# First layer's spatial products in other banks, newest norm first, last token tiles one by one

## The chip, the cores and the metric

The kernel runs on one core of one Trainium2 chip. The metric is the device time of one execution in microseconds (us). A core has five engines with instruction streams of their own: TensorE (PE, with its weight loads PEld), VectorE (DVE), ScalarE (ACT), GpSimd (POOL) and SyncE (SP), which here issues nearly all DMAs. Matmuls write to PSUM, which is dealt out in banks of 128 x 512 float32. VectorE and ScalarE read results from there ("evict" them) and so free the bank for a later matmul.

## The reference, cut to what matters

Sigmoid attention over 4 batches, 12 heads, 448 tokens and head size 64, then two gated layers with a spatial product (d_model 768, two halves of 512 features).

```python
scores = scale * np.matmul(q, k.transpose(0, 1, 3, 2)) - np.log(S)
x = np.matmul(1.0 / (1.0 + np.exp(-scores)), v)      # then heads side by side: (4, 448, 768)

# a gated layer; the first has relu and no g, the second gelu, g and "+ x" around the result
h = act(x @ w_in)                                    # (4, 448, 1024)
u, v = h[..., :512], h[..., 512:]
v_n = (v - mean(v)) / np.sqrt(var(v) + 1e-06) * g    # over the 512 features of a token
v_s = np.einsum('ts,bsd->btd', w_spatial, v_n) + b_spatial[None, :, None]
out = (u * v_s) @ w_out                              # (4, 448, 768)
```

## The kernel before, in words

Float32 products are made of three products of rounded parts: each operand is a high part (written by ScalarE's copy) and a low part (VectorE subtracts the high part from the value), and high x high, high x low, low x high are added up in one PSUM bank.

The work on TensorE has these stages, in the order of the program: attention; the first layer, batch by batch; a product of the first layer's `w_out` and the second layer's `w_in` ("merge", in place of two products later); the second layer, batch by batch. In a layer a batch b goes through

- `hv(b, j)` for 4 token tiles (3 in odd batches; the rests of 64 tokens of two batches share one tile): the v half of h, for 128 tokens and 512 features. 18 matmuls of 512 columns in the first layer, 12 in the second. ScalarE evicts the bank with the activation (L594), VectorE takes mean and variance (L597, L598), GpSimd makes 1/sqrt (L599, L602). The rest, `norm`, is put on a list of jobs, `chain`.
- `norm` (a generator): at its second tick VectorE applies mean and factor (L608) and ScalarE copies the high part (L616, or L622 for the tile of rests); at its third tick VectorE makes the low part (L618, L625).
- `hu(b, i)` for 4 blocks of 128 features: the u half, turned, 12 matmuls of 448 columns in the second layer and 18 in the first; ScalarE evicts (L639).
- `sp(b, i)` for the same 4 blocks: 11 matmuls of the spatial product (L654). In the first layer VectorE adds the bias (L658) and multiplies with u (L660); in the second it does so at L664 and L668, then ScalarE copies the high part (L672) and VectorE makes the low one (L682).
- in the second layer `out(b, i, False)` and `out(b, i, True)`: what x and what block i of the gated product give to the turned output, over six banks (`out_banks`: two pairs "sc" and two banks "av"). In the last batch `out_last` makes the output in token rows instead: three token tiles k = 1, 2, 3, each in a bank of 512 and one of 256 columns, and `rests_first`/`rests_last` make the tile of rests of two batches in the banks "t". `leave` copies a finished token tile out of PSUM and writes it with a DMA.

Banks: `bank()` deals from a pool "t" of two, `av_bank()` from a pool "av" of two, `two_banks()` from a pool "sc" of two pairs. A matmul into a bank waits until the last result there is evicted.

Order: all engines' instructions stand in the order in which this program issues them. After each product a step is made (`fill` in the first layer, `step` in the second). It ticks three belts of jobs: `chain` (the norms and low parts), `spatial` (loads of spatial weights) and `belt` (loads of other weights). `Belt.tick` goes through its running jobs in the order in which they were added, so the oldest norm comes first. In the second layer a step first calls `store`: VectorE transposes one of the six banks of the batch before (L797) and SP writes it out; a batch has six, one per step from its first.

Of the kernel before, what the change touches and what calls it, by code (L numbers as in the profile page):

```python
# [26 lines left out]
def tile_sigmoid_attention_two_gated_mlps(  # L27
# [36 lines left out]
    P = 128  # L64
# [5 lines left out]
    KF = FF // P  # L70
# [22 lines left out]
    def bank():  # L93
        return later["ps_t"].tile([P, 512], F32, tag="t", name="t")

    def two_banks():
        return later["ps_sc"].tile([P, 2, 512], F32, tag="sc", name="sc")

    def av_bank():
        return ps_av.tile([P, 512], F32, tag="av", name="av")  # L100
# [162 lines left out]
    class Belt:  # L263


        def __init__(self):
            self.waiting, self.running = [], []

        def add(self, job):
            self.running.append(job)  # L270

        def tick(self, new=0):
            for job in list(self.running):
                if next(job, self) is self:
                    self.running.remove(job)
            while new and self.waiting:
                job = self.waiting.pop(0)
                next(job)
                self.running.append(job)
                new -= 1  # L280
# [30 lines left out]

    first = pieces_in(l1)
    out1 = pieces_kept(w_out1, 0, rows_of(flat))
    belt, chain, spatial = Belt(), Belt(), Belt()
    spatial.waiting = [load_w_sp(l1, j) for j in range(4)]


# [241 lines left out]
    class Mlp:  # L559
# [82 lines left out]
        def sp(self, b, i):  # L642
            L = self.L
            cols = slice(REST, SPAN) if b % 2 == 0 else slice(0, S)
            fs = slice(i * P, (i + 1) * P)
            ps = av_bank() if L.n == 1 and i % 2 else bank()
            todo = []
            for j in range(3):
                (vh, vl), wh, wl = self.v[j], L.sh[:, j, cols], L.sl[:, j, cols]
                todo += [(vh[:, fs], wh), (vh[:, fs], wl), (vl[:, fs], wh)]  # L650
            vr = self.v[3][b % 2]
            todo += [(vr[:, fs], w[:, 3, cols]) for w in (L.sh, L.sl)]
            for n, (a, w) in enumerate(todo):
                nc.tensor.matmul(ps[:, :S], a, w, start=(n == 0), stop=(n == len(todo) - 1))  # L654
            u = self.u[i]
            t = self.pool.tile([P, S + 16], F32, tag="gt", name="gt", bufs=1)[:, :S]
            if L.n == 1:
                nc.vector.tensor_tensor(out=t, in0=ps[:, :S], in1=L.bb[:, cols], op=ALU.add)  # L658
                o = (b % 2) * S
                nc.vector.tensor_tensor(  # L660
                    out=xs[b // 2][:, i, o:o + S], in0=t, in1=u, op=ALU.mult
                )
                return
            nc.vector.scalar_tensor_tensor(  # L664
                out=t, in0=ps[:, :S], scalar=L.gc[:, i:i + 1], in1=L.bb[:, cols],
                op0=ALU.mult, op1=ALU.add,
            )
            nc.vector.tensor_tensor(out=u, in0=t, in1=u, op=ALU.mult)  # L668
            whole, rest = self.parts(b)
            gh = self.pool.tile([P, S], F32R, tag="gh", name="gh", bufs=2)  # L670
            gl = self.pool.tile([P, S], F32R, tag="gl", name="gl", bufs=2)
            nc.scalar.copy(out=gh[:, whole], in_=u[:, whole])  # L672
            self.g[i] = gh, gl
            if rest:
                if b % 2 == 0:
                    self.rests[i] = stg.tile([P, 2, P], F32R, tag="f", name="gr", bufs=4)
                at = REST * (b % 2)
                rh, rl = [self.rests[i][:, x, at:at + REST] for x in range(2)]
                nc.scalar.copy(out=rh, in_=u[:, rest])

            def low():
                nc.vector.tensor_tensor(  # L682
                    out=gl[:, whole], in0=u[:, whole], in1=raw(gh[:, whole]), op=ALU.subtract
                )
                if rest:
                    nc.vector.tensor_tensor(out=rl, in0=u[:, rest], in1=raw(rh), op=ALU.subtract)
                yield

            chain.add(low())
# [44 lines left out]

        ends = slice(0, 512), slice(512, DM)

        def out_last(self, b, i, second):


            if not second and i == 0:  # L740
                self.out_banks()
            pair = self.g.pop(i) if second else self.x[b][i]
            done = second and i == KF - 1
            for k in range(1, 4):
                at = REST + (k - 1) * P
                bs = self.o[2 * (k - 1):2 * k]
                for ps, cols in zip(bs, self.ends):
                    self.rows(ps, [x[:, at:at + P] for x in pair], i, second, cols)
                    if done and k == 3:
                        self.leave(k, [(ps, cols)], ((out[b, (k - 1) * P:k * P], slice(0, P)),))  # L750
                if done and k < 3:
                    row = out[b, (k - 1) * P:k * P]
                    self.leave(k, zip(bs, self.ends), ((row, slice(0, P)),), both=k)

        def rests_first(self, b):

# [80 lines left out]
    with tc.manual_schedule():  # L837
# [23 lines left out]
        with tc.tile_pool(name="fpool", bufs=1) as fpool:  # L861
# [106 lines left out]
            for b in range(B):  # L968
                last = b == B - 1
                stores = list(range(KD)) if b else []  # L970

                def step(new=0, waits=False):
                    if stores:
                        m2.store(b - 1, stores.pop(0))
                    fill(0 if b else new, waits)

                def split_next(c):
                    if not last:
                        m2.split_x(b + 1, c, c + 1)

                out_part = m2.out_last if last else m2.out
                for j in range(4 - b % 2):
                    m2.hv(b, j)
                    step(1)
                for i in range(KF):
                    m2.hu(b, i)
                    step(2)
                m2.sp(b, 0)
                step(1, True)
                m2.sp(b, 1)  # L990
                step(1, True)
                out_part(b, 0, False)
                split_next(0)
                step(1)
                out_part(b, 0, True)
                split_next(1)
                step(1)
                m2.sp(b, 2)
                step(0, True)
                out_part(b, 1, False)  # L1000
                split_next(2)
                step(1)
                out_part(b, 1, True)
                split_next(3)
                step()
                m2.sp(b, 3)
                step(0, True)
                out_part(b, 2, False)
                step()
                out_part(b, 2, True)  # L1010
                out_part(b, 3, False)
                if last:
                    m2.rests_first(b)
                    m2.rests_last(b)
                out_part(b, 3, True)


# [33 lines left out]
```

## Time and profile before

| | |
|---|---|
| Median of 3 runs | 563.37 us (563.28 to 563.59) |
| The profiled execution | 563.3 us |
| Its span, first to last instruction | 561.5 us |
| TensorE busy | 552.6 us, 98% of the span |
| VectorE busy | 367.7 us, 65% |
| ScalarE busy | 231.8 us, 41% |
| GpSimd busy | 30.3 us, 5% |
| Mean granted TensorE clock | 0.999 |

TensorE's row of busy time includes the drain of each matmul, which overlaps the next matmul, so its length says less than the distance between the starts of two matmuls. In a timeline the bracket behind a row is the idle time of its engine before it and what ended it. The chain of waits lists what the last instruction had to wait for, in order of time; "issue" pieces are left out below.

### The profile page before, as it was taken

How to read it: one execution, taken by the hardware profiler on the slowest of the kernel's cores; microseconds unless marked ns; L12 is line 12 of the kernel's file. 1: busy time of each engine (PE TensorE's matmuls, PEld its weight loads, DVE VectorE, ACT ScalarE, POOL GpSimd, SP SyncE). 2: the span in 40 equal slices, each digit the busy share in tenths (PEclk: the TensorE clock that was granted, in tenths of full speed). 3: DMA queues.
4: the chain of work that ended last, by engine and by line, in shares of the span. 5: the costliest groups of instructions: out<-in, count | busy, mean ns of one | idle time of the engine just before them, and what ended most of it. 6: DMA issues, size and time to landing. Idle time of an engine off the chain costs nothing.

```text
span 561.5 us, 9207 instructions
## 1 busy us (share of the span) xinstructions
PE 552.6 (98%) x3484; PEld 438.1 (78%) x3484; DVE 367.7 (65%) x835; ACT 231.8 (41%) x389; POOL 30.3 (5%) x62
## 2 busy tenths in 40 slices
PE   8999999999999999999999999999999999999996
PEld 6444444444799898897998888998999879989885
DVE  5999999875589799889774977942541264225211
ACT  6878878876342261351542245311320132112001
POOL 0000000000110200200100020001000110010000
PEclk9999999999999999999999999999999999999999
DMA  7868677533044265552545534101500140014003
GB/s 221 234 188 229 166 223 211 150 68 72 4 139 132 68 171 119 128 144 87 160 143 121 140 116 127 58 0 19 81 1 0 22 78 1 1 20 66 0 1 112
DMA packets 96893, 56.45 MB, mean 101 GB/s; under 512 B 67537, under 2 KB 84049, under 8 KB 96849
## 3 DMA queue, kind: packets, MB, share of 16 engines
q1 hardware_dynamic: 96704, 55.60, 37.9%
q8 instruction: 27, 0.44, 0.3%
q10 hardware_dynamic: 144, 0.26, 0.1%
q14 instruction: 18, 0.14, 0.1%
HBM read 44.83 MB, written 11.01 MB: 99 GB/s over the span
## 4 chain that ended last, share of the span: by engine, by line
PE 93%; DVE 2%; ACT 2%; DMA 1%; issue 0%; SPq 0%; DVEq 0%
PE t L634 16%; PE t L588 15%; PE av L457 13%; PE sc L720 10%; PE t L654 9%; PE sc L423 9%; PE av L720 5%; PE av L654 3%; PE sc L730 3%; PE t L814 3%; PE av L814 3%; PE sc L441 2%; PE t L730 1%; PE av L730 1%; DMA inq<-in_q_dram 1%; DVE st L597 1%
## 5 line engine op out<-in xcount | busy, mean ns | idle before, releaser
L408 ACT ACTIVATE a<-sc,small 128x896 f32<-128x896 f32 x72 | 68.6, 1007 | 20.5 <-PE sc L423 20.5
L597 DVE BATCH_NORM_STATS2 st<-vr 128x6 f32<-128x512 f32 x28 | 19.4, 694 | 67.4 <-ACT vr L594 67.4
L457 PE MATMUL av<-a,vt 128*64 128x448 f32 x288 | 63.2, 554 | 0.0
L423 PEld LDWEIGHTS sc<-opq,opk 32*128 32x128 f32 x864 | 40.2, 183 | 26.3 <-issue 8.5
L423 PE MATMUL sc<-opq,opk 32*128 32x448 f32 x864 | 55.4, 378 | 0.2 <-ACT opq L382 0.2
L594 ACT ACTIVATE vr<-t 128x512 f32<-128x512 f32 x28 | 16.7, 597 | 90.9 <-PE t L588 87.6
L654 PE MATMUL t<-sh,v 128*128 128x448 f32 x168 | 49.2, 362 | 0.0
L588 PE MATMUL t<-vh,xh 128*128 128x512 f32 x112 | 41.6, 391 | 0.7 <-ACT vr L594 0.7
L457 PEld LDWEIGHTS av<-a,vt 128*64 128x64 f32 x288 | 17.0, 136 | 31.9 <-issue 28.4
L664 DVE SCALAR_TENSOR_TENSOR gt<-t,bb 128x448 f32<-128x448 f32 x16 | 10.9, 682 | 46.1 <-PE t L654 46.1
L672 ACT CAST gh<-u 128x448 fp32r<-128x448 f32 (+1 forms) x16 | 8.6, 540 | 71.6 <-DVE u L668 71.6
L588 PE MATMUL t<-vh,xl 128*128 128x512 f32 x98 | 38.1, 389 | 0.0
L599 POOL TENSOR_SCALAR st<-st 128x1 f32<-128x1 f32 x28 | 10.7, 382 | 473.9 <-DVE st L598 473.9
L634 PE MATMUL t<-xh,uh 128*128 128x448 f32 x96 | 34.9, 363 | 0.0
L634 PE MATMUL t<-xh,ul 128*128 128x448 f32 x96 | 34.8, 362 | 0.0
L654 PE MATMUL t<-sl,v 128*128 128x448 f32 x96 | 34.7, 362 | 0.0
L634 PE MATMUL t<-xl,uh 128*128 128x448 f32 x96 | 34.6, 360 | 0.0
L654 PEld LDWEIGHTS t<-sh,v 128*128 128x128 f32 x168 | 31.5, 187 | 2.0
L616 ACT CAST v<-vr 128x512 fp32r<-128x512 f32 x24 | 14.9, 621 | 43.8 <-DVE vr L608 43.8
L588 PE MATMUL t<-vl,xh 128*128 128x512 f32 x84 | 32.7, 389 | 0.0
L182 DVE SCALAR_TENSOR_TENSOR f<-w,f 128x256 uint32<-128x256 uint32 x72 | 30.6, 425 | 2.5
L188 DVE SCALAR_TENSOR_TENSOR f<-w,f 128x256 int32<-128x256 int32 x72 | 30.6, 425 | 2.4
(196 smaller groups left out, 1253.8 us busy)
## 6 DMA issues: line engine op xcount, KB each, us to landing
w<-in_moe_w_in_dram SPq DMA_DIRECT2D x48, 256.0 KB, 3.5
w<-in_moe_w_out_dram SPq DMA_DIRECT2D x24, 256.0 KB, 3.1
ink<-in_k_dram SPq DMA_DIRECT2D x12, 448.0 KB, 5.9
inq<-in_q_dram SPq DMA_DIRECT2D x12, 448.0 KB, 7.4
vt<-in_v_dram SPq DMA_DIRECT2D x48, 96.0 KB, 6.6
out_dram<-y SPq DMA_DIRECT2D x48, 56.0 KB, 1.9
flat<-f SPq DMA_DIRECT2D x18, 128.0 KB, 1.7
w<-flat SPq DMA_DIRECT2D x12, 192.0 KB, 2.4
```

The lines of the kernel that those rows point to most:

```text
L182: nc.vector.scalar_tensor_tensor(out=f.bitcast(U32), in0=low.bitcast(U32), scalar=29, in1=f.bitcast(U32), op0=ALU.logical_shift_right, op1 ...
L188: nc.vector.scalar_tensor_tensor(out=f, in0=high, scalar=-0x40000000, in1=f, op0=ALU.bitwise_and, op1=ALU.bitwise_or)
L408: nc.scalar.activation(a[:, 2 * x:2 * x + 2], sc[x][:, :, :S], AF.Sigmoid, bias=bias_s, scale=scale)
L423: nc.tensor.matmul(sc[h // 2][:, h % 2, :S], opk[ps, x, o:o + P], opq[ps, y, S * j:S * (j + 1)], start=(t == 0), stop=(t == 5), tile_posit ...
L457: nc.tensor.matmul(avp[n, x][o * D:(o + 1) * D, :S], vt[:, h, r] if r < 3 else vr[ps, o], att[n, r][:, h] if r < 3 else att[n, r][ps, h], ...
L588: nc.tensor.matmul(ps[:, :FF], a, w, start=(c == 0 and n == 0), stop=(c == self.kc - 1 and n == 2),)
L597: nc.vector.bn_stats(out=st, in_=vr)
L634: nc.tensor.matmul(ps[:, :S], w, a, start=(c == 0 and n == 0), stop=(c == self.kc - 1 and n == 2),)
L654: nc.tensor.matmul(ps[:, :S], a, w, start=(n == 0), stop=(n == len(todo) - 1))
L720: nc.tensor.matmul(self.o[m][:, :n_cols], w, a, start=(not second and i == 0 and n == 0), stop=(second and i == KF - 1 and n == 2),)
L730: nc.tensor.matmul(ps[:, :cols.stop - cols.start], a, w, start=(not second and i == 0 and n == 0), stop=(second and i == KF - 1 and n == 2),)
L814: nc.tensor.matmul(ps[:, :FF], x, w[:, c], start=(c == 0 and n == 0), stop=(c == KD - 1 and n == 2),)
```

## The change

Four edits:

- `sp` in the first layer takes "sc" (the first bank of a pair) for blocks 0 and 2, where it took "t"; blocks 1 and 3 take "av" as before. The second layer's `sp` still takes "t".
- `chain` is a `Belt(-1)`: a tick goes through the running jobs from the newest to the oldest.
- `step` in the second layer calls `fill` first and `store` behind it. Two stores stand in the first step of a batch, none in the other steps of `hv`, one in each step of `hu`.
- In the last batch `out_last(b, 3, False)` and the rests come ahead of the last two blocks of the gated product, and these two are taken together, token tile by token tile: tile 1 is finished, then 2, then 3.

```diff
--- before.py
+++ after.py
@@ -263,14 +263,14 @@
     class Belt:
 
 
-        def __init__(self):
-            self.waiting, self.running = [], []
+        def __init__(self, order=1):
+            self.waiting, self.running, self.order = [], [], order
 
         def add(self, job):
             self.running.append(job)
 
         def tick(self, new=0):
-            for job in list(self.running):
+            for job in self.running[::self.order]:
                 if next(job, self) is self:
                     self.running.remove(job)
             while new and self.waiting:
@@ -311,7 +311,7 @@
 
     first = pieces_in(l1)
     out1 = pieces_kept(w_out1, 0, rows_of(flat))
-    belt, chain, spatial = Belt(), Belt(), Belt()
+    belt, chain, spatial = Belt(), Belt(-1), Belt()
     spatial.waiting = [load_w_sp(l1, j) for j in range(4)]
 
 
@@ -643,7 +643,7 @@
             L = self.L
             cols = slice(REST, SPAN) if b % 2 == 0 else slice(0, S)
             fs = slice(i * P, (i + 1) * P)
-            ps = av_bank() if L.n == 1 and i % 2 else bank()
+            ps = bank() if L.n == 2 else av_bank() if i % 2 else two_banks()[:, 0]
             todo = []
             for j in range(3):
                 (vh, vl), wh, wl = self.v[j], L.sh[:, j, cols], L.sl[:, j, cols]
@@ -734,23 +734,25 @@
 
         ends = slice(0, 512), slice(512, DM)
 
-        def out_last(self, b, i, second):
+        def out_last(self, b, i, second, more=()):
 
 
             if not second and i == 0:
                 self.out_banks()
-            pair = self.g.pop(i) if second else self.x[b][i]
-            done = second and i == KF - 1
+            steps = ((i, second), *more)
+            done = steps[-1] == (KF - 1, True)
+            pairs = [self.g[i] if second else self.x[b][i] for i, second in steps]
             for k in range(1, 4):
                 at = REST + (k - 1) * P
+                row = ((out[b, (k - 1) * P:k * P], slice(0, P)),)
                 bs = self.o[2 * (k - 1):2 * k]
                 for ps, cols in zip(bs, self.ends):
-                    self.rows(ps, [x[:, at:at + P] for x in pair], i, second, cols)
+                    for pair, s in zip(pairs, steps):
+                        self.rows(ps, [x[:, at:at + P] for x in pair], *s, cols)
                     if done and k == 3:
-                        self.leave(k, [(ps, cols)], ((out[b, (k - 1) * P:k * P], slice(0, P)),))
+                        self.leave(k, [(ps, cols)], row)
                 if done and k < 3:
-                    row = out[b, (k - 1) * P:k * P]
-                    self.leave(k, zip(bs, self.ends), ((row, slice(0, P)),), both=k)
+                    self.leave(k, zip(bs, self.ends), row, both=k)
 
         def rests_first(self, b):
 
@@ -969,10 +971,11 @@
                 last = b == B - 1
                 stores = list(range(KD)) if b else []
 
-                def step(new=0, waits=False):
-                    if stores:
-                        m2.store(b - 1, stores.pop(0))
+                def step(new=0, waits=False, n=0):
                     fill(0 if b else new, waits)
+                    for c in stores[:n]:
+                        m2.store(b - 1, c)
+                    del stores[:n]
 
                 def split_next(c):
                     if not last:
@@ -981,10 +984,10 @@
                 out_part = m2.out_last if last else m2.out
                 for j in range(4 - b % 2):
                     m2.hv(b, j)
-                    step(1)
+                    step(1, n=0 if j else 2)
                 for i in range(KF):
                     m2.hu(b, i)
-                    step(2)
+                    step(2, n=1)
                 m2.sp(b, 0)
                 step(1, True)
                 m2.sp(b, 1)
@@ -1007,11 +1010,14 @@
                 step(0, True)
                 out_part(b, 2, False)
                 step()
+                if last:
+                    out_part(b, 3, False)
+                    m2.rests_first(b)
+                    m2.rests_last(b)
+                    out_part(b, 2, True, ((3, True),))
+                    continue
                 out_part(b, 2, True)
                 out_part(b, 3, False)
-                if last:
-                    m2.rests_first(b)
-                    m2.rests_last(b)
                 out_part(b, 3, True)
 
 
```

First TensorE, in the first layer around the end of batch 2: the first matmuls of the spatial products of blocks 0 and 2, and of the first three v-products of batch 3, with what they wait for. Before:

```order
L654 MATMUL t_3353<-sh1_1956,v0_3066 128x448 [waits Activation_49]
...
L654 MATMUL t_3394<-sh1_1956,v0_3066 128x448 [waits Activation_49]
...
L588 MATMUL t_3429<-vh1_79,xh_3246 128x512 [waits DVE_49]
...
L588 MATMUL t_3471<-vh1_79,xh_3246 128x512 [waits Activation_49]
...
L588 MATMUL t_3512<-vh1_79,xh_3246 128x512 [waits DVE_49]
```

and in the changed kernel:

```order
L654 MATMUL sc_3353<-sh1_1956,v0_3066 128x448
...
L654 MATMUL sc_3394<-sh1_1956,v0_3066 128x448
...
L588 MATMUL t_3429<-vh1_79,xh_3246 128x512 [waits Activation_49]
...
L588 MATMUL t_3471<-vh1_79,xh_3246 128x512
...
L588 MATMUL t_3512<-vh1_79,xh_3246 128x512 [waits Activation_49]
```

The spatial products are in "sc" and no longer wait at their start; the v-products find in "t" only banks that ScalarE evicts, and the second has no wait of its own left.

Then VectorE in the second layer, batch 2, from the step behind the first v-product on: statistics (L597, L598), the transposes of a turned output (L797; two pieces each, since batch 1 stands in two parts), the norm (L608) and the low half (L618). Before:

```order
L597 BN_STATS st<-vr 128x6
L598 BN_AGGR st<-st 128x2
L797 STREAM_TRANSPOSE y<-sc 128x384
L797 STREAM_TRANSPOSE y<-sc 128x64
L608 TENSOR_SCALAR vr<-vr,st 128x512
L597 BN_STATS st<-vr 128x6
L598 BN_AGGR st<-st 128x2
L797 STREAM_TRANSPOSE y<-sc 128x384
L797 STREAM_TRANSPOSE y<-sc 128x64
L618 TENSOR_TENSOR v_5059<-vr,v_5058 128x512
L608 TENSOR_SCALAR vr<-vr,st 128x512
```

and in the changed kernel (L799 is L797 of before):

```order
L799 STREAM_TRANSPOSE y<-sc 128x384
L799 STREAM_TRANSPOSE y<-sc 128x64
L799 STREAM_TRANSPOSE y<-sc 128x384
L799 STREAM_TRANSPOSE y<-sc 128x64
L597 BN_STATS st<-vr 128x6
L598 BN_AGGR st<-st 128x2
L608 TENSOR_SCALAR vr<-vr,st 128x512
L597 BN_STATS st<-vr 128x6
L598 BN_AGGR st<-st 128x2
L608 TENSOR_SCALAR vr<-vr,st 128x512
L618 TENSOR_TENSOR v_5059<-vr,v_5058 128x512
```

Two transposes of outputs stand behind the first statistics, none in the next steps, and the norm now follows the statistics at once, with the low half behind it.

Last TensorE at the end of the program, the third token tile in its banks `av_5674` (512 columns) and `av_5675` (256); `gh_5727` and `gl` of the same pair are block 2, `gh_5784` block 3. Before:

```order
L730 MATMUL sc_5673<-oh2_4078,gl_5785 128x256
L730 MATMUL av_5674<-oh2_4078,gh_5784 128x512
L730 MATMUL av_5674<-ol2_4079,gh_5784 128x512
L730 MATMUL av_5674<-oh2_4078,gl_5785 128x512
L730 MATMUL av_5675<-oh2_4078,gh_5784 128x256
L730 MATMUL av_5675<-ol2_4079,gh_5784 128x256
L730 MATMUL av_5675<-oh2_4078,gl_5785 128x256
```

and in the changed kernel:

```order
L730 MATMUL av_5674<-oh2_4078,gh_5727 128x512
L730 MATMUL av_5674<-ol2_4079,gh_5727 128x512
L730 MATMUL av_5674<-oh2_4078,gl_5728 128x512
L730 MATMUL av_5674<-oh2_4078,gh_5784 128x512
L730 MATMUL av_5674<-ol2_4079,gh_5784 128x512
L730 MATMUL av_5674<-oh2_4078,gl_5785 128x512
L730 MATMUL av_5675<-oh2_4078,gh_5727 128x256
L730 MATMUL av_5675<-ol2_4079,gh_5727 128x256
L730 MATMUL av_5675<-oh2_4078,gl_5728 128x256
L730 MATMUL av_5675<-oh2_4078,gh_5784 128x256
L730 MATMUL av_5675<-ol2_4079,gh_5784 128x256
L730 MATMUL av_5675<-oh2_4078,gl_5785 128x256
```

A token tile now takes 12 matmuls from its first to its last, where it took 6, and the tiles end twice as far apart. The instructions of ScalarE, GpSimd and SP stand in the same order in both kernels.

## Rows read from the trace of the kernel before

**Rows 1.** The page: busy us, share of the span, instructions.

```profile
PE 552.6 (98%) x3484; PEld 438.1 (78%) x3484; DVE 367.7 (65%) x835; ACT 231.8 (41%) x389; POOL 30.3 (5%) x62
```

**Rows 2.** Table by stage: first u-product to first spatial product.

```profile
core 0: us, PE busy (x) PEld busy (x) DVE busy (x) ACT busy (x) POOL busy (x), PEclk, DMA share, GB/s
157.93:172.33 14.40, 14.40 (x74) 13.50 (x73) 12.33 (x30) 7.16 (x15) 1.29 (x2) 1.00 0.49 156
336.19:346.70 10.51, 10.09 (x50) 8.85 (x48) 8.26 (x16) 6.86 (x14) 2.00 (x3) 1.00 0.31 86
392.48:402.21 9.73, 9.73 (x49) 8.93 (x48) 5.98 (x11) 3.79 (x7) 0.81 (x3) 1.00 0.59 93
450.74:462.15 11.41, 10.31 (x49) 8.77 (x48) 7.69 (x18) 4.51 (x8) 1.29 (x3) 1.00 0.51 81
504.10:513.92 9.82, 9.82 (x49) 8.92 (x48) 5.83 (x12) 3.79 (x7) 0.85 (x3) 1.00 0.52 82
```

**Rows 3.** Timeline of TensorE, first layer, batch 3: start, us, instruction.

```profile
259.85 0.39 PE L588 MATMUL t<-vh,xl 128*128 128x512 f32 x1
260.92 0.50 PE L588 MATMUL t<-vh,xh 128*128 128x512 f32 x1 [0.69 <-ACT vr L594]
261.26 0.40 PE L588 MATMUL t<-vl,xh 128*128 128x512 f32 x1
```

**Rows 4.** Timeline of TensorE, second layer, batch 2, third u-product.

```profile
457.03 0.47 PE L634 MATMUL t<-xh,vl 128*128 128x448 f32 x1 [1.10 <-ACT u L639]
```

**Rows 5.** Chain of waits, second layer, batch 2, one round: start, us, what.

```profile
448.83 0.51 ACT vr L594
...
450.30 0.71 DVE y L797 x2
451.01 0.57 DVE v L618
...
452.60 0.60 ACT vr L594
```

**Rows 6.** Chain of waits, second layer, batch 0.

```profile
325.43 5.50 PE t L588 x24
...
337.54 0.50 ACT vr L594
...
338.98 0.57 DVE v L618
...
341.08 0.45 ACT u L639
```

**Rows 7.** Chain of waits, last batch, token tiles 1 and 2.

```profile
553.25 2.10 PE sc L730 x12
```

**Rows 8.** Timeline, last matmul and last copy.

```profile
556.11 0.28 PE L730 MATMUL av<-oh,gl 128*128 128x256 f32 x1
556.42 0.42 DVE L780 COPY x<-av 128x256 f32<-128x256 f32 x1
```

**Rows 9.** Table by stage, behind TensorE's end (columns of rows 2).

```profile
557.30:560.20 2.90, 0.00 (x0) 0.00 (x0) 0.00 (x0) 0.00 (x0) 0.00 (x0) 0.95 0.87 333
560.20:561.50 1.30, 0.00 (x0) 0.00 (x0) 0.00 (x0) 0.00 (x0) 0.00 (x0) 0.50 0.00 0
```

**Rows 10.** DMA issues from 556.6 on: count, KB each, median us to landing.

```profile
out_dram<-x SPq DMA_DIRECT2D x1, 128.0 KB, 3.6
```

**Rows 11.** DMA issues from 553.0 to 554.6, the tile of rests.

```profile
out_dram<-x SPq DMA_DIRECT2D x2, 192.0 KB, 2.9
```

**Rows 12.** The page, DMA issues: stores of turned outputs in mid-kernel.

```profile
out_dram<-y SPq DMA_DIRECT2D x48, 56.0 KB, 1.9
```

**Rows 13.** Chain of waits, second layer, batch 0: first product of a gated block.

```profile
354.86 2.40 PE sc L720 x12
```

**Rows 14.** Timeline of VectorE, the low half that this product reads.

```profile
353.03 0.62 DVE L682 TENSOR_TENSOR gl<-u,gh 128x448 fp32r<-128x448 f32 x1
```

**Rows 15.** Timeline, first layer, batch 2: third spatial product; first one's sum read.

```profile
251.57 0.36 PE L654 MATMUL t<-sh,v 128*128 128x448 f32 x1
...
254.31 0.62 DVE L658 TENSOR_TENSOR gt<-t,bb 128x448 f32<-128x448 f32 x1
```

## The prediction

> **What bounds the kernel now.** The page comes first: TensorE is busy 98% of the span [rows 1], and the change removes no matmul. So only three things can be won: stretches in which TensorE stands still, what lies ahead of its first matmul, and what lies behind its last. The change touches nothing ahead of the first matmul. The rest I looked for with the waits of TensorE, and priced from the starts of its matmuls in the timeline, since a row's idle time leaves out what a wait costs around itself.
>
> The measure is the pace. The 72 u-products of batch 0 of the first layer take 14.40 us [rows 2], so a matmul of 448 columns starts every 0.200 us when nothing holds it. In the second layer each batch has 48 such products from its first u-product to its first spatial product, 9.60 us at that pace. They take 10.51, 9.73, 11.41 and 9.82 us [rows 2], which is 0.91, 0.13, 1.81 and 0.22 us too much: 3.07 us in all. In the first layer there is one hole, at the second v-product of batch 3: the starts go 259.85, 260.92, 261.26 [rows 3] where two steps of 0.23 would be due, so 1.41 − 0.46 = 0.95 us.
>
> What ends each wait? In the first layer it is ScalarE's eviction (L594) of the v-product just before [rows 3]. There are two banks "t", so this product was handed the very bank that its neighbour had just filled; the other one was still held by a spatial product whose sum VectorE reads late. In the second layer it is ScalarE's eviction L639 of the first u-products [rows 4], there the longest. ScalarE is not busy, it is late: the chain of waits goes round ScalarE and VectorE. In batch 2 one round lasts from 448.83 to 452.60, 3.77 us [rows 5]; in batch 0 from 337.54 to 341.08, 3.54 us [rows 6]. TensorE makes two v-products in 5.50 us, one per 2.75 [rows 6]. So in each round the evictions fall behind by 1.0 and 0.8 us, and after three or four rounds two banks no longer cover that.
>
> **The change part by part.**
>
> *Spatial products of the first layer into "sc" and "av".* The ring "t" then serves products that ScalarE evicts at once, and the waits in the order agree: the second v-product of batch 3 no longer waits for anything of its own. Gain 0.95 us. The "sc" pairs are idle in this layer, so nothing else is displaced. Bounds: 0 (the pool repeats itself) and 0.95; I take 0.95, since the wait is gone from the order.
>
> *Newest norm first, stores behind.* A round in batch 2 holds the transpose of a turned output (L797, 0.71 us) and the low half of an older norm (L618, 0.57 us) between the statistics and the norm L608 that ScalarE's cast waits for [rows 5]. Both move behind L608: 3.77 − 0.71 − 0.57 = 2.49 us per round, under the 2.75 of TensorE. The eviction is then paced by TensorE and nothing of the wait is left. Two stores now stand in one step, behind the first v-product: 2 x 0.71 = 1.42 us on VectorE, in a step of 2.75 in which the first batch of statistics takes under 1 us, so they end before the next eviction. Batches 1 and 3 have the same round with a shorter transpose. In batch 0 there are no stores, and 3.54 − 0.57 = 2.97 us stays above 2.75, but two low halves come out ahead of the first u-eviction, 1.14 us, where TensorE waited about 0.7 and then 0.2. So it arrives in time by some 0.4 us; that eviction is what is late next. Sum over the second layer: 3.07 us. Bounds: nothing gained if the round were held by something not on the chain, 3.07 at most. I take 2.95, with 0.1 for a wait that stays just visible in batch 0, the round that is still slower than TensorE.
>
> What moves with it: the low halves (L618) come 0.47 to 0.6 us later. Their reader is the first spatial product, four u-products (9.6 us) behind, so that is covered. The norm of the fourth tile may now stand at VectorE's head waiting for GpSimd's two small operations; behind it wait a store and two low halves, with the same cover. The last store of a batch moves from the second or third u-product to the fourth; the output product that wants its bank back starts two spatial products (2 x 11 x 0.200 = 4.4 us) later. SP's order of transfers is the same as before. Cost of all of this: 0.
>
> *Last batch, tile by tile.* No matmul is added, so TensorE's end moves only with the stalls. Before, the rest tile ends, then 12 matmuls in 2.10 us finish two token tiles [rows 7] and six more the third: four tiles of 384 KB are to be written within 3 us of each other. The last matmul starts at 556.11, the last copy ends at 556.84 [rows 8], but the transfers run until 560.2: the 16 DMA engines move 333 GB/s at a share of 0.87 with TensorE already done [rows 9]. The last piece, 128 KB, needs 3.6 us from issue to landing [rows 10], where 192 KB issued into empty queues need 2.9 [rows 11] and a 56 KB store in mid-kernel 1.9 [rows 12]. After the change the rest tile leaves two products earlier (6 us ahead of the end instead of 3), and the three tiles are 2.1 us apart instead of 1.05. One tile takes about 1.2 us at 333 GB/s, so the queues are drained when the last tile comes. Its last piece then lands as fast as an uncontended one: between 1.9 and 2.9 us after issue, a gain of 1.7 to 0.7, and not below nothing, as no piece of the last tile is issued later than before. The 56 and 192 KB rows put 128 KB at about 2.4, but the 192 KB are two halves of partitions issued back to back, which delays the second; nearer 2.2. I take 1.4. The copies ahead of the issue cost what they did (0.42 us on VectorE [rows 8]).
>
> The Trainium skill, page "DMA: Bandwidth & Descriptors", section "Anatomy of one DMA — SWDGE (gpsimd) path", gives a DMA a fixed 2.0 us, mostly the receipt of the write, plus its bytes at 436 GB/s. It was measured on another issuing path; as an estimate it makes 2.3 us of 128 KB, so 1.3 us of the 3.6 can go however early the other tiles leave, and the total would be 558.1. The 56 KB row, 1.9, lies a little under its 2.1.
>
> **Sum.** 0.95 + 2.95 + 1.4 = 5.3 us. The profiled execution took 563.3 us (span 561.5), 0.1 us from the median of the runs, 563.37. 563.3 − 5.3 = 558.0 us.
>
> **Rivals.**
> - *The tail gives nothing.* If the last landing is bound by latency and not by the transfers ahead of it, only the stalls go: 563.3 − 3.9 = 559.4. For it: every DMA here takes at least 1.9 us. Against: 3.6 for 128 KB, beside a share of 0.87.
> - *The stalls move instead of going.* TensorE comes to the second layer's first output product nearly 2 us earlier. It starts there at 354.86 [rows 13], and the low half of its operand ends at 353.65 [rows 14], 1.2 us ahead; VectorE was late there behind a weight piece that SP had fetched. If the fetches don't come forward with TensorE, up to 0.7 us is handed back; and if the wait in batch 0 stays as it is (0.91), 1.6 in all: 559.6. Against: these fetches are issued when VectorE frees a buffer, in the steps that get faster.
> - *The pool deals "sc" as it dealt "t".* This is the slower side. VectorE reads a spatial product's sum late: in batch 2 the third spatial product starts at 251.57, and the first one's sum is read from 254.31 on, to 254.93 [rows 15]. If the third product got the pair that the first had filled, TensorE would wait 3.4 us there; the other three batches read earlier, I put them at about a third of it each, so some 7 us in all: 563.3 − 5.3 + 7 = 565.0. It decides from the point where more than 5.3 us are lost. For it: exactly that happened with "t". Against: in the order no third spatial product waits for VectorE on its first matmul, which it would have to.
> - *It doesn't do what it says* (the hole in the first layer stays): 559.0; within the range.
>
> **How the numbers follow.** Forecast 0.72, tail gives nothing 0.10, stalls handed back or the first-layer hole left 0.12 (a sixth of that with nearly all lost, so no change), "sc" dealt twice 0.03, something unseen 0.03 (no change). A measurement of this kernel tells 0.2% (1.1 us) from no change. Faster 0.92, same 0.05, slower 0.03. The likeliest case alone spans 557.3 (the tail at its best, 1.7, and all 4.0 of the stalls) to 558.9 (0.7, and 0.3 of the stalls left). The range goes on to the two milder rivals: 557.3 to 560.2.
>
> **What would show it.** In the profile after: the four stretches from first u-product to first spatial product take 9.6 to 9.7 us each; TensorE waits for no eviction from the first layer on; the round in batch 2 lasts 2.75 us, paced by TensorE; the last 128 KB land 2 to 2.5 us after issue, and from the last matmul to the end of the span it is about 3.7 us instead of 5.0. Wrong would be: a wait of L654 for VectorE (the "sc" rival), a wait of L720 or L730, or a last landing that still takes over 3 us with the other tiles gone.

## The result and the profile after

| | before | after |
|---|---|---|
| Median (range), 5 runs each | 563.59 us (563.28 to 564.26) | 558.08 us (557.10 to 558.42) |
| Ratio, 95% interval | | 0.9896 (0.9881 to 0.9910) |
| Profiled execution, its span | 563.3, 561.5 us | 558.1, 556.3 us |

Faster by 5.5 us, 1.0%, with an interval that is clear of no change. The forecast was 558.0.

The page after; columns as in [rows 1]:

```profile
PE 551.0 (99%) x3484; PEld 439.4 (79%) x3484; DVE 366.9 (66%) x835; ACT 233.1 (42%) x389; POOL 32.6 (6%) x62
```

The same number of matmuls. Two cuts of the span show where the time went: at the start of the first layer's first v-product, and at the start of the last matmul. Before, by stage (span from : to, its length, then each engine's busy time, the granted clock, DMA share, GB/s):

```profile
141.32:556.11 414.79, 412.59 (x2022) 369.53 (x2020) 247.45 (x539) 121.95 (x250) 29.65 (x56) 1.00 0.29 73
556.11:561.48 5.37, 0.28 (x3) 0.07 (x1) 0.71 (x2) 0.54 (x1) 0.00 (x0) 0.86 0.69 243
```

After, by the same cuts:

```profile
141.92:552.60 410.68, 410.68 (x2021) 370.06 (x2020) 246.86 (x539) 123.65 (x250) 31.91 (x56) 1.00 0.30 75
552.60:556.31 3.71, 0.28 (x3) 0.07 (x1) 0.42 (x1) 0.20 (x1) 0.00 (x0) 0.98 0.56 212
```

The middle lost 4.11 us and TensorE is now busy in all of it; the end lost 1.66. The stretch ahead of the first v-product, which the change doesn't touch, came out 0.60 longer, so the span shrank by 5.17. More on that 0.60 below.

The four stretches from first u-product to first spatial product in the second layer, by stage; they answer to [rows 2]:

```profile
335.83:345.44 9.61, 9.61 (x50) 9.00 (x49) 8.16 (x16) 6.68 (x14) 1.99 (x3) 1.00 0.35 99
391.21:400.81 9.60, 9.60 (x49) 9.00 (x48) 5.81 (x11) 3.49 (x7) 1.47 (x3) 1.00 0.41 65
449.31:458.92 9.61, 9.61 (x50) 9.00 (x49) 6.93 (x17) 4.10 (x8) 1.77 (x3) 1.00 0.27 43
500.86:510.46 9.60, 9.60 (x49) 9.00 (x48) 5.54 (x11) 3.49 (x7) 1.47 (x3) 1.00 0.39 62
```

All at the pace of 0.200 us per product. The waits of TensorE over the whole span (line waited for: us, times, longest):

```profile
PE av L521 <- POOL ident masks.py:199: 1.3, 1, 1.3
PE av L457 <- DMA vt<-in_v_dram: 0.4, 1, 0.4
```

Both lie in the first 12 us. No wait for an eviction is left. At the second v-product of the first layer's batch 3, TensorE's timeline has no bracket where [rows 3] had 0.69 us of idle time; the starts are one step apart:

```profile
260.47 0.39 PE L588 MATMUL t<-vh,xl 128*128 128x512 f32 x1
260.70 0.39 PE L588 MATMUL t<-vh,xh 128*128 128x512 f32 x1
260.92 0.39 PE L588 MATMUL t<-vl,xh 128*128 128x512 f32 x1
```

ScalarE's timeline in batch 2 of the second layer, which answers to [rows 5]:

```profile
444.07 0.60 ACT L594 ACTIVATE vr<-t 128x512 f32<-128x512 f32 x1 [2.12 <-PE t L588]
...
446.80 0.60 ACT L594 ACTIVATE vr<-t 128x512 f32<-128x512 f32 x1
...
449.56 0.60 ACT L594 ACTIVATE vr<-t 128x512 f32<-128x512 f32 x1
...
452.10 0.54 ACT L639 ACTIVATE u<-t 128x448 f32<-128x448 f32 x1
```

The evictions come 2.73, 2.76 and 2.54 us apart, not 3.77: TensorE's own pace. The chain of waits says the same; where it went round ScalarE and VectorE, it is now TensorE alone:

```profile
438.58 10.90 PE t L588 x48
449.48 9.60 PE t L634 x48
```

The end: the chain's last matmuls and copy, which answer to [rows 7, 8]:

```profile
546.58 4.20 PE sc L730 x24
550.78 2.11 PE av L730 x12
...
552.92 0.42 DVE x L782
```

and the last two DMA issues (KB each, us to landing), which answer to [rows 10]:

```profile
out_dram<-x ACTq DMA_DIRECT2D x1, 256.0 KB, 2.1
out_dram<-x SPq DMA_DIRECT2D x1, 128.0 KB, 1.9
```

The rest tile and the tile before the last now have 2.1 us each to leave, and the last 128 KB lands in 1.9 us, where it took 3.6.

### The profile page after: what moved, and what is told of

Its sections match the earlier page's. It is cut to its first block, busy times and chain, and to the rows that moved or that the text cites. A ratio compares the mean times of both kernels' runs of the same rounds, so it can differ in the third digit from the quotient of the medians.

```text
span 556.3 us, 9214 instructions
## 1 busy us (share of the span) xinstructions
PE 551.0 (99%) x3484; PEld 439.4 (79%) x3484; DVE 366.9 (66%) x835; ACT 233.1 (42%) x389; POOL 32.6 (6%) x62
## 4 chain that ended last, share of the span: by engine, by line
PE 95%; DMA 2%; DVE 2%; SPq 0%; issue 0%
PE t L634 17%; PE t L588 17%; PE av L457 12%; PE sc L720 10%; PE sc L423 8%; PE t L654 6%; PE av L720 5%; PE av L654 3%; PE sc L654 3%; PE sc L730 3%; PE t L816 3%; PE av L816 3%; PE sc L441 2%; PE av L730 2%; PE t L730 1%; DMA vt<-in_v_dram 1%
## 5 line engine op out<-in xcount | busy, mean ns | idle before, releaser
L408 ACT ACTIVATE a<-sc,small 128x896 f32<-128x896 f32 x72 | 68.5, 1006 | 20.2 <-PE sc L423 20.2
L597 DVE BATCH_NORM_STATS2 st<-vr 128x6 f32<-128x512 f32 x28 | 19.4, 694 | 64.6 <-ACT vr L594 64.6
L594 ACT ACTIVATE vr<-t 128x512 f32<-128x512 f32 x28 | 16.7, 598 | 91.7 <-PE t L588 87.9
L588 PE MATMUL t<-vh,xh 128*128 128x512 f32 x112 | 41.5, 391 | 0.0
L588 PE MATMUL t<-vh,xl 128*128 128x512 f32 x98 | 38.1, 389 | 0.0
L654 PE MATMUL t<-sh,v 128*128 128x448 f32 x112 | 32.8, 362 | 0.0
L588 PE MATMUL t<-vl,xh 128*128 128x512 f32 x84 | 32.7, 389 | 0.0
L634 PE MATMUL t<-xh,vl 128*128 128x448 f32 x96 | 29.7, 363 | 0.0
L177 ACT ACTIVATE g<-w 128x256 f32<-128x256 f32 x48 | 19.9, 432 | 19.2 <-DMA w<-in_moe_w_out_dram 12.1
```

The costliest lines, as they stand in the source:

```text
L177: nc.scalar.activation(g, high.bitcast(F32), AF.Square)
L408: nc.scalar.activation(a[:, 2 * x:2 * x + 2], sc[x][:, :, :S], AF.Sigmoid, bias=bias_s, scale=scale)
L588: nc.tensor.matmul(ps[:, :FF], a, w, start=(c == 0 and n == 0), stop=(c == self.kc - 1 and n == 2),)
L634: nc.tensor.matmul(ps[:, :S], w, a, start=(c == 0 and n == 0), stop=(c == self.kc - 1 and n == 2),)
```

## The experiments

The ratio of each row is to the kernel before timed beside it on the same chip (medians 563.54 to 563.82 us). "Middle" and "end" are the two cuts above, from each profiled execution; "stretches" are the four of [rows 2].

| Kernel | median us (range) | ratio to before (95%) | first v-product at | middle | end | stretches, batches 0 to 3 |
|---|---|---|---|---|---|---|
| before | 563.59 | | 141.32 | 414.79 | 5.37 | 10.51 9.73 11.41 9.82 |
| after | 558.08 | 0.9896 | 141.92 | 410.68 | 3.71 | 9.61 9.60 9.61 9.60 |
| e1 banks | 562.69 (561.76–563.41) | 0.9984 (0.9975–0.9993) | 141.12 | 413.75 | 5.34 | 10.5 9.73 11.41 9.83 |
| e2 order in the second layer | 560.81 (560.19–561.33) | 0.9947 (0.9934–0.9959) | 141.97 | 411.68 | 5.37 | 9.6 each |
| e3 end | 562.00 (561.31–563.59) | 0.9966 (0.9954–0.9978) | 143.35 | 414.72 | 3.72 | as before |
| e4 after, one pair twice | 566.40 (564.54–567.01) | 1.0042 (1.0026–1.0059) | 142.02 | 419.37 | 3.72 | 9.6 each |
| e5 newest norm first alone | 561.70 (560.47–562.53) | 0.9959 (0.9943–0.9974) | 142.07 | 412.30 | 5.37 | 9.6 9.6 10.19 9.6 |
| e6 stores behind alone | 561.24 (560.67–562.42) | 0.9958 (0.9944–0.9973) | 141.22 | 412.61 | 5.39 | 10.51 9.6 9.6 9.6 |
| e7 before, last tile's stores only | 561.98 (561.71–563.20) | 0.9969 (0.9957–0.9981) | 141.52 | 415.19 | 3.95 | 10.97 9.73 11.41 9.83 |
| e8 after, last tile's stores only | 557.39 (557.00–557.94) | 0.9884 (0.9867–0.9902) | 140.92 | 410.69 | 3.59 | 9.6 each |
| after, once more | 558.50 (557.33–559.31) | 0.9898 (0.9882–0.9915) | 142.89 | 410.68 | 3.71 | 9.6 each |
| e9 after, values fetched earlier | 557.72 (557.67–557.85) | 0.9888 (0.9873–0.9903) | 141.50 | 410.68 | 3.72 | 9.6 each |

**One part at a time: e1, e2, e3.** The theory says that the three parts add up to 0.95, 2.95 and 1.4 us. The rivals leave one of them at nothing, or have the stalls of one come back in another.

e1 takes only the line of the banks into the kernel before:

```diff
-            ps = av_bank() if L.n == 1 and i % 2 else bank()
+            ps = bank() if L.n == 2 else av_bank() if i % 2 else two_banks()[:, 0]
```

> The kernel before with the bank edit alone: in the first layer blocks 0 and 2 of the spatial product go to "sc". Theory: the hole at the second v-product of batch 3 (0.95 us by the starts of the matmuls) goes and nothing else changes, so about 562.6 us; the four stretches of the second layer keep their 3.07 us of waits or nearly so, and the tail stays at 5.0 to 5.3 us from the last matmul's start to the end of the span. Rival (the hole moves): TensorE waits elsewhere in the first layer or at the merge and the time stays at 563.5.

By stage (columns as above), the middle of e1:

```profile
141.12:554.87 413.75, 412.23 (x2022) 369.72 (x2020) 247.52 (x539) 121.82 (x250) 29.65 (x56) 1.00 0.29 73
```

The middle is 1.04 us shorter, and the wait of L588 for L594 is gone from the list of waits. The stretches of the second layer keep their stalls. No other wait appears.

e2 takes the order alone: the belt of v-tiles runs its newest job first, and the stores stand behind it (cut to the main lines).

```diff
-            for job in list(self.running):
+            for job in self.running[::self.order]:
...
-    belt, chain, spatial = Belt(), Belt(), Belt()
+    belt, chain, spatial = Belt(), Belt(-1), Belt()
...
-                    if stores:
-                        m2.store(b - 1, stores.pop(0))
                     fill(0 if b else new, waits)
+                    for c in stores[:n]:
+                        m2.store(b - 1, c)
+                    del stores[:n]
...
-                    step(1)
+                    step(1, n=0 if j else 2)
...
-                    step(2)
+                    step(2, n=1)
```

> The kernel before with the newest norm first and the stores behind, without the bank edit and the tail. Theory: all four stretches from first u-product to first spatial product take 9.6 us, 3.07 us are gained, about 560.5 us; the hole in the first layer stays, 0.95 us. Rival (the order of VectorE has nothing to do with it, the evictions are late because ScalarE is): less than 1 us gained.

```profile
141.97:553.65 411.68, 410.99 (x2022) 370.18 (x2020) 246.60 (x539) 123.27 (x250) 31.93 (x56) 1.00 0.29 74
```

This row by stage of e2 gives a middle shorter by 3.11 us, and all four stretches at 9.6; the wait in the first layer stays. e3 takes the end alone, with `out_last` as in the change (cut):

```diff
+                if last:
+                    out_part(b, 3, False)
+                    m2.rests_first(b)
+                    m2.rests_last(b)
+                    out_part(b, 2, True, ((3, True),))
+                    continue
...
```

> The kernel before with the last batch's new order alone. Theory: TensorE's waits stay as before (4.0 us in all), the time from the start of the last matmul to the end of the span falls from 5.3 to 3.7 us, so 1.6 us gained, about 561.9 us. Rival (the last landing is bound by latency, not by what is queued ahead): it stays above 5 us and the time at 563.3 or higher.

```profile
143.35:558.07 414.72, 412.51 (x2021) 369.61 (x2020) 247.88 (x539) 122.43 (x250) 29.67 (x56) 1.00 0.29 75
558.07:561.79 3.72, 0.28 (x3) 0.07 (x1) 0.42 (x1) 0.20 (x1) 0.00 (x0) 1.00 0.55 211
```

By these rows of e3 only the end changes, by 1.65 us. The profile of e3 has its wait for L594 and its waits for L639 as before. The three parts together make 1.04 + 3.11 + 1.65 = 5.80 of shorter profile against 5.77 for the whole change (4.11 + 1.66): they add up, and nothing is handed back. The profiled execution of e3 is the slowest of its six timed (563.59), since its first v-product starts only at 143.35: TensorE waits 0.9 us for the first tile of values there, and 0.5 us for ScalarE (L408).

**The slower rival: e4.** The changed kernel, but the third spatial product of the first layer gets the very "sc" pair that the first one filled.

```diff
-            ps = bank() if L.n == 2 else av_bank() if i % 2 else two_banks()[:, 0]
+            if L.n == 1 and i == 0:
+                self.pair = two_banks()
+            ps = bank() if L.n == 2 else av_bank() if i % 2 else self.pair[:, 0]
```

> The changed kernel, but in the first layer the third spatial product of a batch gets the very bank of the first (the slower rival of the prediction, made true). Theory: TensorE waits at the first matmul of the third spatial product of each batch until VectorE has read the first one's sum, 3.4 us in batch 2 and about 1 to 1.3 us in the other three, some 7 us in all, about 565 us. Rival (VectorE's late reading is itself an effect of the banks and comes earlier once TensorE waits, or the time is given back by later waits that vanish): 560 us or less.

The waits of TensorE that this adds (us in all, times, longest):

```profile
PE sc L656 <- DVE gt L660: 6.0, 4, 2.9
```

One per batch, as the rival said. The middle is 8.69 us longer than in the changed kernel, though the waits add up to 6.0. The timeline of TensorE behind the longest wait, in batch 2, shows where the rest is:

```profile
258.06 0.61 PE L656 MATMUL sc<-sh,v 128*128 128x448 f32 x1 [2.92 <-DVE gt L660]
258.47 0.58 PE L656 MATMUL sc<-sl,v 128*128 128x448 f32 x1
```

and a table by stage, of two stretches behind it (after the busy times: the granted clock):

```profile
258.05:261.45 3.40, 3.39 (x9) 3.01 (x10) 3.37 (x6) 0.62 (x1) 0.00 (x0) 0.53 0.58 173
261.50:265.00 3.50, 3.50 (x18) 3.19 (x17) 2.50 (x5) 0.00 (x0) 0.00 (x0) 0.98 0.00 0
```

Behind the long wait the granted clock is 0.53 for 3.4 us, close to the 1.2 GHz level; products start every 0.37 us there instead of every 0.20. That is ten steps with some 1.7 us too much. Without this 1.7 the 8.69 are 7.0, the four waits counted from start to start. The waits of 0.8 to 1.4 us in the other batches leave the clock where it was; in batch 0 TensorE's timeline has

```profile
178.19 0.47 PE L656 MATMUL sc<-sh,v 128*128 128x448 f32 x1 [0.76 <-DVE gt L660]
178.50 0.36 PE L656 MATMUL sc<-sl,v 128*128 128x448 f32 x1
```

The loss of clock does not come in every run: of e4's four, the two longer (566.89, which was profiled, and 567.01) show a mean granted clock of 0.997, the two shorter (565.90 and 564.54) one of 1.000. By the medians, which bank the pool hands out is worth 8.3 us here (566.40 against 558.08), more than the whole change gains, and e4 is slower than before.

**Which of the two moves does it: e5 and e6.** e5 has only the newest norm first (the lines of e2's diff down to `Belt(-1)`), e6 only the stores behind (the lines after that).

> The kernel before with the newest norm first alone; a store still stands ahead of the norm in each step. Theory (the round through both engines sets the evictions, and two banks hide what it falls behind): batch 0 gains its 0.9 us; in batch 2 the first u-eviction comes 2 x 0.57 = 1.14 us earlier where TensorE waited 1.3, so 0.2 to 0.4 us stay of the 1.8; batches 1 and 3 gain theirs. First v-product to last matmul falls by about 2.8 us, time about 560.8 us. Rival (each part brings its own share, 0.57 of 1.28 us per round): about 1.5 us gained.

> The kernel before with the stores behind the jobs of the step alone; the oldest norm still comes first. Theory: batch 0, which has no stores, keeps its 0.9 us; in batch 2 three transposes of 0.71 us leave the rounds ahead of the first u-eviction, 2.1 us where 1.3 were missing, so its 1.8 us go; batches 1 and 3 gain theirs. First v-product to last matmul falls by about 2.2 us, time about 561.4 us: together with the newest norm alone more than both edits bring at once (3.1). Rival (each part brings its own share): about 1.6 us gained, and the two parts add up to 3.1.

By stage, what is left in e5 is in batch 2:

```profile
450.45:460.64 10.19, 9.90 (x49) 8.85 (x48) 7.57 (x18) 4.62 (x8) 1.75 (x3) 1.00 0.53 83
```

and in e6 in batch 0:

```profile
336.12:346.63 10.51, 10.09 (x50) 8.86 (x49) 8.25 (x16) 6.86 (x14) 1.99 (x3) 1.00 0.29 87
```

Alone they take 2.49 and 2.18 us from the middle, together 3.11. They overlap in batches 1 and 3, where either is enough, and in most of batch 2. Batch 0 has no stores, so there only the norm's order counts. In batch 2 the turned output that e5 leaves ahead of the norm keeps the round too long; ScalarE's timeline of e5:

```profile
445.21 0.60 ACT L594 ACTIVATE vr<-t 128x512 f32<-128x512 f32 x1 [2.12 <-PE t L588]
...
448.45 0.59 ACT L594 ACTIVATE vr<-t 128x512 f32<-128x512 f32 x1
...
451.87 0.60 ACT L594 ACTIVATE vr<-t 128x512 f32<-128x512 f32 x1
...
455.12 0.54 ACT L639 ACTIVATE u<-t 128x448 f32<-128x448 f32 x1
```

Rounds of 3.24, 3.42 and 3.25 us against 2.75 fall behind by about 0.5 us each, and 0.59 us of that comes through the two banks to TensorE. My price for e5 (0.2 to 0.4 left) was a little too low; e6 came out as expected.

**Is the end held by the transfers ahead of it: e7 and e8.** Both leave out the writing of the last batch's rest tile and its first two token tiles to the output; the copies and the last tile's two transfers stay. e7 does it to the kernel before, e8 to the changed one.

```diff
             queue = nc.scalar if len(parts) == 1 and cols.start == 0 else nc.sync
+            if len(parts) > 1:
+                return
```

> The kernel before, which at the end writes the third token tile of the last batch alone: the transfers of the tile of rests and of token tiles 1 and 2 are left out (their copies stay). Theory (the last piece waits for what is queued on the DMA engines): the last 128 KB land about 2 us after issue and the time from the start of the last matmul to the end of the span falls from 5.4 to 3.7 us or a little less, about 561.8 us. Rival (it is the order of matmuls and copies that made the tail short in the change): it stays at 5.4 us.

> The changed kernel, which at the end writes the third token tile of the last batch alone; the transfers of the tile of rests and of token tiles 1 and 2 are left out (their copies stay). Theory (with tiles 2.1 us apart the queues are drained): nothing or next to it is left to gain, the tail stays at 3.6 to 3.7 us, about 558 us. Rival (the second tile is still in the way of the third): the tail falls by 0.5 us or more.

The end of e7 by stage, and then its last DMA issue:

```profile
556.71:560.66 3.95, 0.28 (x3) 0.07 (x1) 0.72 (x2) 0.55 (x1) 0.00 (x0) 0.83 0.26 100
```

```profile
out_dram<-x SPq DMA_DIRECT2D x1, 128.0 KB, 2.2
```

The end of e8 by stage:

```profile
551.61:555.20 3.59, 0.28 (x3) 0.07 (x1) 0.42 (x1) 0.19 (x1) 0.00 (x0) 1.00 0.29 110
```

Without the other tiles the end of the kernel before goes from 5.37 to 3.95 with no matmul moved: 1.42 of the 1.66 was waiting behind their transfers. In the changed kernel leaving them out gives 0.12, so the change has taken nearly all there is. The rest, 0.36 between e7 and e8, is mostly the landing (2.2 us against 1.9, the last DMA issue of e8),

```profile
out_dram<-x SPq DMA_DIRECT2D x1, 128.0 KB, 1.9
```

and goes with the distance of the last tile's own two transfers, which the new order of matmuls also changes. Timelines of the other engines: in e7

```profile
557.29 0.37 ACTq L788 DMA_DIRECT2D out_dram<-x  x1
557.48 0.35 SPq L788 DMA_DIRECT2D out_dram<-x  x1
```

and in e8

```profile
551.83 0.37 ACTq L790 DMA_DIRECT2D out_dram<-x  x1
...
552.38 0.35 SPq L790 DMA_DIRECT2D out_dram<-x  x1
```

The 256 KB half leaves 0.19 us ahead of the last 128 KB in e7, 0.55 us ahead in e8. That this distance makes the 0.3 us of landing is likely, not shown by a run of its own. (The 10.97 of batch 0 in e7 is a variation of that run: nothing there was edited.)

**The start, with the first values fetched earlier: e9.** The changed kernel run again repeats from the first v-product on (410.68 and 3.71 us); what differs lies ahead: its first v-product starts at 142.89, against 141.92. TensorE's timeline of that run shows two waits, 1.02 us in all, where the first profile had one of 0.39:

```profile
11.56 0.97 PE L457 MATMUL av<-a,vt 128*64 128x448 f32 x4 [0.62 <-DMA vt<-in_v_dram]
...
23.00 1.50 PE L423 MATMUL sc<-opq,opk 32*128 32x448 f32 x22 [0.40 <-ACT a L408]
```

The first tile of values is fetched behind two pairs of q and k. e9 puts its four large transfers ahead of the second pair, and its small ones behind (cut):

```diff
         load_qk(0)
+        rest_of_v = load_v(0)
         load_qk(1)
-        load_v(0)
+        rest_of_v()
...
```

> The changed kernel with the first value tile's four transfers issued ahead of the second pair of q and k, which are not needed until later. Theory: in the profiles TensorE waits 0.4 to 0.9 us for that tile in some runs (it was issued behind 1.8 MB of q and k); with it earlier the wait goes, 0 to 0.9 us gained by run, about 0.4 us in the median, 557.6 us, and less spread. Rival (the second q and k, later by as much, are waited for instead, or the first q lands later): no gain or a loss of up to 1 us.

The first score product of e9 in TensorE's timeline:

```profile
7.18 4.39 PE L429 MATMUL sc<-opq,opk 32*128 32x448 f32 x48 [1.51 <-ACT opq L388]
```

It starts 0.47 us later than in the changed kernel (6.71), and the wait for the values is gone. e9's median is 0.8 us below that of the changed kernel run beside it (0.4 was expected), and its four runs lie within 0.18 us, where those of the changed kernel spread over 2. The best runs of the changed kernel (557.10, 557.33) are still faster than any of e9. So by its one profile e9 pays 0.5 us at the start, as its rival said, for a wait that varies by run (0.39 us, then 0.62 and 0.40 in the two profiles of the changed kernel, nothing in e8); with intervals of the ratio that overlap (0.9873 to 0.9903 and 0.9882 to 0.9915) it is at best a small gain.

## Why the prediction was right

- *First-layer hole, 0.95.* Measured 0.95 at the hole and 1.04 over e1's middle. "The pool repeats itself" fell with it: the spatial products wait for nothing.
- *Second layer, 2.95 of 3.07.* The four stretches went from 41.47 to 38.42 us, 3.05; e2's middle lost 3.11. The 0.1 that I left for batch 0 did not stay. The round there is indeed still slower than TensorE; ScalarE's timeline has its last rounds at 2.93 and 2.94 us (forecast 2.97):

```profile
333.55 0.59 ACT L594 ACTIVATE vr<-t 128x512 f32<-128x512 f32 x1
...
336.48 0.59 ACT L594 ACTIVATE vr<-t 128x512 f32<-128x512 f32 x1
...
339.42 0.54 ACT L639 ACTIVATE u<-t 128x448 f32<-128x448 f32 x1
```

  The first u is out at 339.96. The third u-product, due 24 products behind 335.83, starts at 340.63: in time by 0.67 us, where I had said 0.4.
- *GpSimd's wait ahead of the fourth tile's norm.* It came, and was hidden. VectorE's timeline in batch 2:

```profile
452.60 0.55 DVE L608 TENSOR_SCALAR vr<-vr,st 128x512 f32<-128x512 f32 x1 [0.46 <-POOL st L602]
```

- *The end, 1.4 (0.7 to 1.7).* This is the term that was mis-sized: it is 1.66, near the upper end, because the last 128 KB lands in 1.9 us and not in the 2.2 that I had chosen between the 56 and the 192 KB rows. There was no need to choose: the page of the kernel before has stores of just this size in mid-kernel (to a scratch tensor in DRAM),

```profile
flat<-f SPq DMA_DIRECT2D x18, 128.0 KB, 1.7
```

  which also goes against my "at least 1.9" for every DMA. And the 2.2 is what e7 has with the last tile's halves 0.19 us apart; that the change sets them 0.55 apart was not in my account. The page "DMA: Bandwidth & Descriptors" of the Trainium skill, section "Anatomy of one DMA — SWDGE (gpsimd) path", puts a fixed 2.0 us and the bytes at 436 GB/s on a DMA, which made my estimate of 2.3 us. It was measured on another path, and on SP's queue the trace does not agree: 1.9 us in the changed kernel and in e8, less than the fixed part alone; the measurement decides. My "5.0 instead of 3.7" for the end mixed two starting points: from the start of the last matmul it went from 5.37 to 3.71, from its end (0.28 us later) from 5.09 to 3.43. That 3.7 was met so closely is luck.
- *The stalls handed back at the first output product.* Not so. TensorE now starts it at 353.60 (the chain of waits), 1.26 us earlier than in [rows 13], and VectorE's low half moved with it:

```profile
352.14 0.62 DVE L682 TENSOR_TENSOR gl<-u,gh 128x448 fp32r<-128x448 f32 x1
```

  It ends at 352.76, 0.84 us ahead; in [rows 13, 14] the margin was 1.21. The fetches came forward, not quite as far as TensorE.
- *The slower rival.* The mechanism is real (e4); only the pool doesn't deal that way. Its place was right, and so was its price of 7 us for the waits alone, 7.0 from start to start; in the profiled execution another 1.7 came from the clock, with which I had not reckoned.
- *The sum.* The parts are 1.04 + 3.11 + 1.65 = 5.8 us, 0.5 more than the 5.3 forecast. The median moved by 5.5, and the profiled span by 5.17, because its first v-product came 0.60 later. TensorE's wait for the first values is 0.4 to 0.6 us in the two profiles of the changed kernel; it is also there in e3 and e5, whose edits lie far behind it, and not in before, e1, e2, e4, e6, e7 and e8. Whether the change makes it more frequent is not shown, nor that it makes up the difference in the medians. The forecast also set out from the profiled 563.3, while the median of before beside the result was 563.59. So that 558.0 came within 0.1 us of 558.08 is in part luck: small errors cancel.
- *The range.* Its lower end was added up wrongly: 563.3 − 1.7 − 4.0 is 557.6, not 557.3. Its upper end, 560.2, lies 0.6 above the dearer of the two rivals that it was to reach (559.4 and 559.6). The result lies within it either way.

## What to carry to other kernels

Where a ring of two buffers stalls an engine that is otherwise full, compare the round of the engines that empty it with the pace of the engine that fills it; in each in-order queue put the one instruction that closes the round first, and the gain ends where the round meets the pace. Price such a wait from start to start of the matmuls, not by its idle time: [rows 3] show 0.69 us of idle time for 0.95 us lost, and e4 6.0 for 7.0, or 8.7 with the clock. At the end of a kernel ask how many bytes are still queued when the last piece is issued, and move matmuls so that the pieces come out evenly.

## What the runs showed of the hardware

- Behind one wait of 2.92 us TensorE's granted clock was 0.53 for 3.4 us, and then full again; ahead of it the engine had run its products 0.20 us apart at full clock (e4's profile; two of its four runs show no such loss in their mean clock). Behind waits of 0.76, 0.97 and 1.36 us it stayed at 1.00.
- Behind a wait at full clock the next matmul, too, started 0.11 us late: 0.31 for 0.20 us in e4's batches 0, 1 and 3, 0.34 for 0.23 in [rows 3]. It is part of what an idle time doesn't tell.
- With little queued ahead, 128 KB landed in 1.7 us (the page of before, mid-kernel) to 1.9 (the end of the changed kernel) and 256 KB in 2.1, against 1.9 for the 56 KB of [rows 12]: between these sizes such a store cost almost the same. Close behind a 256 KB store 128 KB took 2.2 (e7), and behind whole tiles 3.6 [rows 10].
